# Turning q' and k' of the last four pairs with the DMA crossbar instead of TensorE

## Chip, cores, metric

One core of a Trainium2 chip. The metric is the device time of one execution in microseconds (us); lower is better. Only one core runs, so there are no dies to compare, and all runs told of here are of the fast state but one of four of e6_loaded. Before: 192.79 us (median of 3, 192.6 to 192.91).

## The reference

A gated linear recurrence over 768 steps for 4 batches of 8 heads (head size 48), then a two-layer MLP (384 to 2048 to 384) with the tanh form of gelu on its 3072 rows:

```python
for t in range(S):
    state = alpha[:, :, t, :, None] * state + np.einsum('bhd,bhe->bhde', k[:, :, t], v[:, :, t])
    y[:, :, t] = np.einsum('bhd,bhde->bhe', q[:, :, t], state)
x = y.transpose(0, 2, 1, 3).reshape(B * S, H * D)
h = x @ w_in
g = 0.5 * h * (1.0 + np.tanh(c * (h + 0.044715 * h * h * h)))
out = g @ w_out
```

## The kernel before

The steps are cut into 6 chunks of 128, the batches into 2 twos: 12 "pairs" of (chunk, two batches), numbered 0 to 11. For a pair, ScalarE takes log alpha (`la`), TensorE sums it along the chunk (`cum`), ScalarE takes exponentials (`b`, `binv`), VectorE forms q' = q b (`qp`) and k' = k binv (`kp`). The kernel turns both, so that head size lies on the partitions, before TensorE forms the scores (`at`). VectorE masks them (`atm`), TensorE forms `y` (`yps`), which is copied (`x`), turned (`xT`) and goes through the MLP (`hT`, gelu into `gT`, `acc`, `ot`, store). A list scheduler in the kernel sets the order of instructions on each engine when it is built, from a table `W` of supposed durations.

```python
    TURN_QK, TURN_X = (), ()
    BUFS = dict(ca=1, yk=2, ff=4, la=3, qp=3, kp=3, b8=2, qkT=3, atm=6, x=3, ot=6, bend=6, a=4, q=4, k=4, v=6)
...
    def turn(self, u, i, which):                     # TensorE: 8 transposes for one batch's q' and k'
        ...
            for j, n in enumerate(which):
                for p in range(H // 2):
                    nc.tensor.transpose(ps[:, j, p, :], u[n + "p"][:, i, 2 * p:2 * p + 2, :].rearrange(
                        "t h d -> t (h d)"), self.ident)
    def turned(self, u, i, which): ...               # VectorE: PSUM to qkT
    def turn_dma(self, u, n):                        # the crossbar: q' or k' of both batches at once
        def emit(e):
            self.nc.sync.dma_start_transpose(
                self.qkT(u)[:, "qk".index(n)].rearrange("d i p t -> d (i p) t"),
                u[n + "p"].rearrange("t i h d -> t (i h d)"))
...
            if m in self.TURN_QK:                    # in tasks(), pair m
                tq = [s.add("turn", {"SP": W["turn"]}, P + 10, self.turn_dma(u, n), d, xbar=W["xbar_qk"]) for n, d in (("q", qp), ("k", kp))]
                owner, turned = tq[0], tq
            for j in range(2):
                ...
                at = s.add("attn", {"PE": W["attn"]}, o + 1, self.attn(u, j), turned)   # waits for all of `turned`
```

## Time and profile before

| Share of the 191.0 us span | busy | instructions |
|---|---|---|
| TensorE (matmul) | 95% | 1919 |
| ScalarE | 71% | 300 |
| VectorE | 58% | 232 |

The profile's span is about 2 us less than the time of a run (191.0 us here, 192.79 the run). The profile's lines, and how to read them, are in the prediction below. The short of it is that TensorE runs with next to no gap from about 30 us to 187 us (from 112 us on no wait of its matmuls is listed), and the DMA engines are full until about 110 us and then nearly idle (200 GB/s from 30 to 110 us, 30 GB/s from 118 to 186).

### The profile page before, as it was taken

How to read it: one execution, taken by the hardware profiler on the slowest of the kernel's cores; microseconds unless marked ns; L12 is line 12 of the kernel's file. 1: busy time of each engine (PE TensorE's matmuls, PEld its weight loads, DVE VectorE, ACT ScalarE, POOL GpSimd, SP SyncE). 2: the span in 40 equal slices, each digit the busy share in tenths (PEclk: the TensorE clock that was granted, in tenths of full speed). 3: DMA queues.
4: the chain of work that ended last, by engine and by line, in shares of the span. 5: the costliest groups of instructions: out<-in, count | busy, mean ns of one | idle time of the engine just before them, and what ended most of it. 6: DMA issues, size and time to landing. Idle time of an engine off the chain costs nothing.

```text
span 191.0 us, 4655 instructions
## 1 busy us (share of the span) xinstructions
PE 181.4 (95%) x1919; PEld 131.8 (69%) x1922; DVE 111.2 (58%) x232; ACT 135.8 (71%) x300; POOL 63.8 (33%) x67
## 2 busy tenths in 40 slices
PE   5887899999999999999999999999999999999992
PEld 1343688656687787786786786786786786785860
DVE  7268650279695794793793883892892950850000
ACT  2544989743868878878778788788688788881931
POOL 7993433896547564655502400000000000000000
PEclk9999999999999999999999999999999999999999
DMA  6999999999999999999998770200200201101101
GB/s 129 181 179 171 207 202 228 182 180 227 249 210 182 164 241 178 181 253 173 187 246 165 152 185 0 84 2 3 82 0 6 80 3 40 42 3 43 45 13 70
DMA packets 38005, 24.68 MB, mean 129 GB/s; under 512 B 27968, under 2 KB 34624, under 8 KB 37984
## 3 DMA queue, kind: packets, MB, share of 16 engines
q0 software_dynamic: 32464, 19.27, 72.5%
q1 hardware_dynamic: 5520, 5.11, 9.1%
q8 instruction: 15, 0.25, 0.6%
q14 instruction: 6, 0.05, 0.1%
HBM read 25.17 MB, written 4.72 MB: 156 GB/s over the span
## 4 chain that ended last, share of the span: by engine, by line
PE 75%; DMA 17%; POOL 4%; issue 1%; DVE 1%; ACT 1%; POOLq 0%; DVEq 0%
PE acc L412 29%; PE hT L398 28%; DMA k<-in_k_dram 9%; DMA w_out<-in_moe_w_out_dram 8%; PE qkT_ps L289 5%; PE at L325 3%; PE yps L374 2%; PE yps L371 2%; PE kv L342 2%; PE xT_ps L388 2%; PE cum L252 2%; POOL q L220 1%; PE cum L254 1%; POOL a L220 1%; POOL k L220 1%
## 5 line engine op out<-in xcount | busy, mean ns | idle before, releaser
L404 ACT ACTIVATE gT<-hT 128x256 bf16<-128x256 f32 x192 | 64.5, 385 | 16.3 <-PE hT L398 15.6
L398 PE MATMUL hT<-xT,w_in 128*128 128x256 bf16 x576 | 71.6, 273 | 0.1
L412 PE MATMUL acc<-w_out,gT 128*128 128x384 bf16 x384 | 68.6, 326 | 0.0
L398 PEld LDWEIGHTS <-w_in 128*128 128x128 bf16 x576 | 53.6, 98 | 8.1 <-issue 0.4
L412 PEld LDWEIGHTS <-gT 128*128 128x128 bf16 x384 | 35.9, 98 | 20.2
L332 DVE TENSOR_TENSOR atm<-at,ut 128x512 bf16<-128x512 f32 x48 | 30.9, 686 | 4.8 <-PE at L325 3.2
L278 DVE TENSOR_TENSOR qp<-q,b 128x768 bf16<-128x768 f32 (+1 forms) x13 | 11.6, 896 | 33.2 <-ACT b L270 33.2
L419 ACT COPY ot<-acc 128x384 f32<-128x384 f32 x16 | 7.7, 478 | 19.0 <-PE acc L412 19.0
L220 POOL DMA_DIRECT2D a<-in_alpha_dram x12 | 13.3, 1110 | 15.3 <-ACT la L241 8.8
L220 POOL DMA_DIRECT2D q<-in_q_dram x13 | 14.6, 1122 | 11.5 <-DVE qp L278 3.6
L220 POOL DMA_DIRECT2D v<-in_v_dram x13 | 14.4, 1111 | 8.0 <-PE hT L398 1.9
L303 DVE COPY qkT<-qkT_ps 128x1024 bf16<-128x1024 bf16 (+1 forms) x22 | 13.8, 663 | 5.5 <-PE qkT_ps L289 5.5
L220 POOL DMA_DIRECT2D k<-in_k_dram x13 | 14.5, 1113 | 7.3 <-DVE xT L392 2.0
L198 ACT ACT_TABLE_LOAD x10 | 12.8, 1283 | 0.9 <-PEq L627 0.7
L241 ACT ACTIVATE la<-a 128x768 f16<-128x768 f32 (+1 forms) x13 | 10.3, 794 | 3.9 <-DMA a<-in_alpha_dram 3.7
L404 ACT ACT_TABLE_LOAD x10 | 12.8, 1283 | 0.2
L270 ACT ACTIVATE b<-cum 128x768 bf16<-128x768 f32 (+1 forms) x13 | 9.9, 762 | 4.1 <-PE cum L254 3.7
L207 PE MATMUL idle<-zero 128*128 128x512 bf16 x31 | 11.2, 483 | 1.4 <-DVE zero L594 1.2
L359 DVE TENSOR_TENSOR st<-stmp,bend 64x192 bf16<-64x192 f32 x32 | 11.3, 353 | 2.1 <-ACT gT L404 0.5
L278 DVE TENSOR_TENSOR kp<-k,binv 128x768 bf16<-128x768 f32 (+1 forms) x15 | 11.7, 792 | 0.6 <-DMA k<-in_k_dram 0.5
L392 DVE COPY xT<-xT_ps 128x384 bf16<-128x384 bf16 x24 | 8.5, 354 | 5.0 <-PE xT_ps L388 5.0
L357 DVE TENSOR_TENSOR stmp<-kv,st 64x192 f32<-64x192 f32 x32 | 11.2, 351 | 0.2
(43 smaller groups left out, 166.8 us busy)
## 6 DMA issues: line engine op xcount, KB each, us to landing
out_dram<-ot SPq DMA_DIRECT2D x24, 192.0 KB, 4.0
q<-in_q_dram POOLq DMA_DIRECT2D x11, 384.0 KB, 13.1
k<-in_k_dram POOLq DMA_DIRECT2D x11, 384.0 KB, 13.0
a<-in_alpha_dram POOLq DMA_DIRECT2D x10, 384.0 KB, 13.0
v<-in_v_dram POOLq DMA_DIRECT2D x11, 192.0 KB, 12.6
w_in<-in_moe_w_in_dram POOLq DMA_DIRECT2D x4, 384.0 KB, 11.8
w_out<-in_moe_w_out_dram POOLq DMA_DIRECT2D x4, 384.0 KB, 15.2
a<-in_alpha_dram SPq DMA_DIRECT2D x1, 384.0 KB, 4.1
```

Source lines behind the costliest of these rows:

```text
L198: nc.scalar.add_instruction(mybir.InstLoadActFuncSet(name=nc.get_next_instruction_name(), act_func_set_id=i, engine=mybir.EngineType.Activ ...
L207: self.nc.tensor.matmul(ps, self.zero[:, 0:self.C], self.zero, start=True, stop=True)
L220: (nc.sync if e == "SP" else nc.gpsimd).dma_start(u[n][:, lo:hi].rearrange("t b h d -> t (b h) d"), src)
L241: self.nc.scalar.activation(u["la"][:, lo:hi, :, 0:self.D], u["a"][:, lo:hi], AF.Ln)
L278: self.nc.vector.tensor_tensor(u[n + "p"][:, lo:hi, :, 0:self.D], u[n][:, lo:hi], u["b" if n == "q" else "binv"][:, lo:hi], op=ALU.mult)
L303: self.copy(e)(t, u.pop(("T_ps", i, which)))
L332: self.nc.vector.tensor_tensor(u["atm", i][:, o], u["at", i][:, o], self.ut[:, None, :].to_broadcast([self.C, self.H // 2, self.C]), op=AL ...
L357: nc.vector.tensor_tensor(s[ps], acc, old[ps, :, fs], op=ALU.add)
L359: nc.vector.tensor_tensor(new[ps, :, fs], acc, u["bend"][ps, i, :, None].to_broadcast([64, H // 2, D]), op=ALU.mult)
L398: self.nc.tensor.matmul(h, self.w_in[:, j, nt * self.C:(nt + 1) * self.C], self.xT[c][:, j, lo:hi].rearrange("p g t -> p (g t)"), start=j ...
L404: return lambda e: self.nc.scalar.activation(self.gT[c % self.NG][:, nt, lo * self.C:hi * self.C], f.pop(("h", c, lo, nt)), AF.Gelu_apprx_ ...
L412: self.nc.tensor.matmul(f["acc", c, b], self.gT[c % self.NG][:, nt, b * self.C:(b + 1) * self.C], self.w_out[:, nt, :], start=nt == 0, sto ...
```

## The change

Intent: take the last four pairs' 64 transposes from TensorE, the bound, and give them to DMA engines that stand idle by then.

```diff
-    TURN_QK, TURN_X = (), ()
+    TURN_QK, TURN_X = (8, 9, 10, 11), ()
```

The scheduler then makes another order: it puts the scores later, where it supposes that the transfers have landed.

## The prediction

> **What bounds the kernel now.** I read first the page's busy shares and the picture in 40 slices, then the chain of work that ended last, cut to the stretches around the last pairs, then the waits, and last the timeline of one pair. The page:
>
> ```profile
> span 191.0 us, 4655 instructions
> PE 181.4 (95%) x1919; PEld 131.8 (69%) x1922; DVE 111.2 (58%) x232; ACT 135.8 (71%) x300; POOL 63.8 (33%) x67
> PE   5887899999999999999999999999999999999992
> PEclk9999999999999999999999999999999999999999
> DMA  6999999999999999999998770200200201101101
> ```
>
> TensorE is full from about slice 7 to the last one, at full clock. The DMA engines are full up to about slice 23 (110 us) and nearly idle after it. So from 110 us on an instruction taken from TensorE should be worth its issue interval, and a transfer finds free engines. Whether TensorE's busy time is useful work is another matter, so I look at the chain, here around the tenth pair (pair 9; columns: start, us, what):
>
> ```profile
> 132.91 0.08 PE cum L254 x4
> 132.98 2.62 PE acc L412 x16
> 135.60 0.33 PE hT L398 x3
> 135.93 0.89 PE qkT_ps L289 x16
> 136.83 0.65 PE hT L398 x6
> 137.48 0.33 PE at L325 x8
> ```
>
> The pieces follow one another without a gap; the 16 transposes of q' and k' hold TensorE 0.89 us, and nothing in them waits. The stretches of the table by windows over just these four groups agree (0.89, 0.90, 0.89, 0.90). In the list of waits from 112 us to the end TensorE's matmuls have no entry at all. The bound is TensorE's instruction stream, in its order.
>
> [...] This trace shows 219 ns for one from start to modelled end, but back to back they cost 0.89/16 = 56 ns each, and that is what removing one gives back. [...] The trace of before has no crossbar transfer[...]. What it has is the output store, 192 KB from the same queue: median landing time in the DMA view, under load and at rest:
>
> ```profile
> out_dram<-ot SPq DMA_DIRECT2D x1, 192.0 KB, 6.9
> ...
> out_dram<-ot SPq DMA_DIRECT2D x2, 192.0 KB, 1.9
> ```
>
> The first is from 92 to 100 us, with loads running; the second from 140 to 160 us. Pair 8's q' is made at 119.7 us in the timeline, after the loads have drained, so all four pairs fall into the second state.
>
> **The change part by part.** *Removed from TensorE:* four pairs of 16 transposes, 0.89 + 0.90 + 0.89 + 0.90 = 3.58 us, all on the path: 192.79 - 3.58 = 189.21 us if nothing else moves. *Removed from VectorE:* eight evictions of 681 ns, 5.4 us. VectorE is 58% busy, so this is worth nothing by itself; in exchange it takes some output copies from ScalarE in the new order. *Added:* two transfers of 256 KB for each pair on SyncE's queue, which otherwise issues only stores (332 ns each). *Moved:* both halves of a pair now wait for both transfers, so the scheduler puts the scores (at) later. In the built order of the changed kernel, pair 8 has cum, 16 acc, 3 hT, 8 kv, 33 hT, then at.
>
> The budget of the transfer, from the timeline of pair 8:
>
> ```profile
> 116.74 0.84 ACT L241 ACTIVATE la<-a 128x768 f16<-128x768 f32 x1
> ...
> 118.86 0.81 ACT L270 ACTIVATE b<-cum 128x768 bf16<-128x768 f32 x1
> ...
> 119.71 0.96 DVE L278 TENSOR_TENSOR qp<-q,b 128x768 bf16<-128x768 f32 x1 [2.29 <-ACT b L270]
> ...
> 120.58 0.95 DVE L278 TENSOR_TENSOR kp<-k,binv 128x768 bf16<-128x768 f32 x1
> ```
>
> q' is ready at 120.67, k' at 121.53. The cum ends at 118.83. By the new order TensorE reaches at after acc 2.62 + hT 0.33 + kv 0.45 + hT 33 x 0.109 = 3.60, so at 125.83. The crossbar has 5.16 us from q', 4.30 us from k'. Pair 9: y 0.37 + xT 0.17 + acc 0.65 + xT 0.17 + acc 2.62 + hT 0.33 + kv 0.45 + hT 3.60 = 8.36 us after cum; but VectorE first has two x (0.56), two xT (0.36) and an output copy (0.56) to do, the last xT being ready at +1.36, so q' is done at about +3.5: 4.9 us left. Pairs 10 and 11 have no kv but 39 hT (4.25): 8.23 - 3.5 = 4.7 us left.
>
> [...] The scheduler's own table supposes 4.95 us, which tells how closely it has placed the scores, not how long a transfer takes. I charge 0.3 us in all for pairs 9 to 11.
>
> *A second small wait:* the next pair's cum. It needs la, which comes after the last gelu and a table load. In before la ends at 117.58, 2.57 us after the last hT (115.01), and cum starts 3.31 us after it: 0.74 us of slack. In the new order only acc 0.65 + at 0.33 + y 0.37 + acc 1.30 = 2.65 us lie between, so the slack is 0.08 us[...]. I charge 0.1 us for each of pairs 9, 10 and 11. Sum: 189.21 + 0.3 + 0.3 = 189.8 us, 1.6% less.
>
> **Rivals.** *A, the crossbar is late:* the wait on the transfers replaces the transposes. Each us that both transfers take over about 4.9 costs nearly 4 us in all, since TensorE takes its instructions in order and the at of every pair stands in the stream. At 6 us, 193.6; the gain is lost at 5.8 us. [...] *B, nothing shows:* ScalarE becomes the bound, because 12 hT groups now run without other matmuls between. In the tail of before 16 gelus take 5.25 us beside 48 hT of 5.24 us, so both go at one rate and B costs only the few tenths already charged. *C, load collisions:* a transfer issued under load would take about 7 us, as the store did, and cost 2 us for a pair. The last load is issued at 108.06 and the engines fall silent near 114 us; the four pairs come later, so I give it little. *D, more than the transposes is gained,* by an emptier VectorE. TensorE has no waits on VectorE after 112 us that could go, so time under 188.9 us has no source that I can see.
>
> **Range and chances.** The floor is the full removal, 189.2, with 0.2 for spread: low 189.0. The upper end is rival A with each pair 0.9 us over budget: 189.2 + 3.6 + 0.3 = 193.1, rounded to 193.0. Two per cent less is 188.93, below the floor, so faster gets 0.05. Two per cent more is 196.65, which takes a crossbar of about 6.8 us a pair: 0.08. Within 2%: 0.87.
>
> **What would show it.** Right: L289 falls from 192 to 128 transposes; eight transfers of 256 KB on SyncE's queue land in 2 to 4.5 us; PE's waits on them are under 0.3 us a pair; the PE line keeps its 9s; the at of pair 8 starts about 7.0 us after its cum ends. The cum wait would show as PE waiting for ACT la by about 0.1 us, three times. Wrong: at starts later than 8.5 us after the cum, with DMA qkT as the releaser, gaps of equal size in all four pairs (rival A) or only in the first (C); or gT as the releaser of acc or hT (B). I would be most wrong if SyncE needs several us to issue one transfer, since k' queues behind q' and the stores behind both.

The sum came to 189.8 us: 192.79 less 3.58 for the transposes, plus 0.3 for late transfers in pairs 9 to 11, plus 3 x 0.1 for the cum's waits. Both charges stand as estimates; so does "land in 2 to 4.5 us" among the signs (the eight took 3.1 to 5.0). Rival A rests on TensorE keeping its order. The trace of the changed kernel shows that: TensorE stood for 0.79 us before pair 8's scores, with 12 hT behind them, while ScalarE sat idle for 1.24 us waiting for those hT.

## The result

The changed kernel took 190.34 us (median of 4, 190.03 to 190.5) beside 192.69 us for the kernel before on the same chip; the ratio is 0.9878 (95% interval 0.9858 to 0.9898). Ratios here are the mean of one kernel's runs over the mean of the other's runs of the same rounds, so they are not quite the ratios of the medians. Executions over 1.5% slower than the fastest of the same kernel are left out of the means. Results are correct. Run again on another chip it took 190.04 us (190.03 to 190.44), ratio 0.9869 (0.9857 to 0.9882).

The page of the changed kernel, the lines that answer to those of before:

```profile
span 188.2 us, 4536 instructions
PE 177.0 (94%) x1858; PEld 127.4 (68%) x1858; DVE 109.6 (58%) x231; ACT 133.1 (71%) x293; POOL 63.7 (34%) x67
PE   5778899999999999999999999989999999999992
DMA  6999999999999999999999790290350430701101
```

TensorE's line keeps its 9s except for one slice, the 27th (122 to 127 us), and the DMA line has new work from there on. The 27th slice is pair 8. The chain of work there (start, us, what), and then the same place of pair 9:

```profile
122.00 4.29 DMA qkT<-kp
126.28 0.05 issue
126.33 0.40 PE at L325 x8
...
135.74 0.34 PE kv L342 x8
136.08 3.60 PE hT L398 x33
139.69 0.33 PE at L325 x8
```

In pair 8 the chain runs through the transfer of k', and the scores start when it lands. In pair 9 the scores follow the last hT at once, but by a margin of only 0.2 us: its k' landed at 139.47. The waits from 112 us on (engine, line, what was waited for: us in total, times, longest):

```profile
PEld L325 <- DMA qkT<-kp: 1.3, 2, 1.1
PE at L325 <- DMA qkT<-kp: 0.8, 1, 0.8
```

One wait of TensorE, 0.8 us (0.79 in the timeline), in pair 8 alone. The transfers themselves are in SyncE's timeline (start, us of issue), pairs 8 and 10:

```profile
120.55 1.35 SPq L308 DMA_TRANSPOSE qkT<-qp  x1
122.00 1.34 SPq L308 DMA_TRANSPOSE qkT<-kp  x1
...
147.72 1.24 SPq L308 DMA_TRANSPOSE qkT<-qp  x1
149.05 1.29 SPq L308 DMA_TRANSPOSE qkT<-kp  x1
```

and in the DMA view (us from the start of the issue to landing), first for 120 to 127 us, then for 147 to 153 us:

```profile
qkT<-qp SPq DMA_TRANSPOSE x1, 5.0
qkT<-kp SPq DMA_TRANSPOSE x1, 4.3
...
qkT<-qp SPq DMA_TRANSPOSE x1, 3.2
qkT<-kp SPq DMA_TRANSPOSE x1, 3.1
```

So the pair that is late issued its transfers no later than the others after its cum (q' 1.9 us after it, pairs 9 and 10 3.0 us); they took 1.2 to 1.8 us longer. To see where the time of the whole kernel went, I measured in every profile the **stretch** from the start of the last cum group of pair 8 to the start of the last output copy, which leaves out the head of the kernel (its loads differ by some tenths from run to run) and its end: before 187.33 - 118.75 = 68.58 us, changed 184.53 - 118.56 = 65.97 us. That is 2.61 us less, where 3.58 us of transposes went: 0.79 us is the wait, 0.18 us the rest.

**Why one pair of four?** Each packet on the DMA queues is in the trace. Between 121.8 and 125.8 us, two things fall together: the 2,048 packets of 256 bytes of q' and k', and at 123.5 us one packet of 16,384 bytes on the queue that the page calls "instruction" (q8). The 17 packets of the transfer that were in flight then took 1,271 to 1,552 ns, against some 20 ns in the mean otherwise, and from 124.0 to 125.2 us hardly any started. (The q8 packet itself ended at 124.5 us; why the hold outlasts it, no run shows.) These packets go with TensorE's instructions (matmuls and weight loads): from the start of one to the start of the next, TensorE starts 198 to 292 of them in the trace of before and 210 to 296 in that of the changed kernel, 251 in the mean in both; of ScalarE's it is 14 to 26, of VectorE's 4 to 18. The page of before has 1919 + 1922 = 3,841 instructions of TensorE and 15 such packets, that of the changed kernel 3,716 and 14. So I take them for fetches of TensorE's instructions, and call them fetches from here on; the trace names the queue, not the engine. Pair 9 was hit too, by a fetch at 134.9 us, and kept its scores in time by the 0.2 us above. My theory after the result, called F: **the gain is 4 x 0.89 us, less a wait in pair 8 that TensorE's own instruction fetch causes by holding the crossbar transfer for 1.2 us or more.** The rivals: U, a loss spread over all pairs (the transfers slow TensorE or VectorE while they run); S, pair 8 is late for a reason of the queue, such as the store behind it.

### The profile page after: what moved, and what is told of

It is laid out like the page before. It is cut to its first block, busy times and chain, and to the rows that moved or that the text cites. A ratio compares the mean times of both kernels' runs of the same rounds, so it can differ in the third digit from the quotient of the medians.

```text
span 188.2 us, 4536 instructions
## 1 busy us (share of the span) xinstructions
PE 177.0 (94%) x1858; PEld 127.4 (68%) x1858; DVE 109.6 (58%) x231; ACT 133.1 (71%) x293; POOL 63.7 (34%) x67
## 4 chain that ended last, share of the span: by engine, by line
PE 72%; DMA 16%; POOL 6%; ACT 1%; issue 1%; DVE 1%; POOLq 0%; DVEq 0%
PE acc L412 29%; PE hT L398 26%; DMA w_out<-in_moe_w_out_dram 8%; DMA a<-in_alpha_dram 6%; PE at L325 4%; PE qkT_ps L289 3%; DMA qkT<-kp 2%; PE yps L371 2%; PE yps L374 2%; PE cum L252 2%; PE xT_ps L388 2%; POOL w_in L228 2%; PE kv L342 1%; POOL q L220 1%; POOL v L220 1%
## 5 line engine op out<-in xcount | busy, mean ns | idle before, releaser
L398 PE MATMUL hT<-xT,w_in 128*128 128x256 bf16 x576 | 69.9, 273 | 0.4 <-DMA w_in<-in_moe_w_in_dram 0.2
L412 PE MATMUL acc<-w_out,gT 128*128 128x384 bf16 x384 | 69.4, 326 | 0.0
L419 ACT COPY ot<-acc 128x384 f32<-128x384 f32 x13 | 6.2, 477 | 15.5 <-PE acc L412 15.5
L381 DVE CAST x<-yps 128x384 bf16<-128x384 f32 x14 | 7.8, 556 | 9.3 <-PE yps L374 9.3
L207 PE MATMUL idle<-zero 128*128 128x512 bf16 x34 | 10.2, 423 | 1.2 <-DVE zero L594 1.2
L325 PE MATMUL at<-qkT 64*128 64x128 bf16 x192 | 9.5, 219 | 1.3 <-DMA qkT<-kp 0.8
```

The source lines that it names most:

```text
L207: self.nc.tensor.matmul(ps, self.zero[:, 0:self.C], self.zero, start=True, stop=True)
L325: nc.tensor.matmul(at[:, o, p, :], t[sl, 1, p, :], t[sl, 0, p, :], start=True, stop=True)
L398: self.nc.tensor.matmul(h, self.w_in[:, j, nt * self.C:(nt + 1) * self.C], self.xT[c][:, j, lo:hi].rearrange("p g t -> p (g t)"), start=j ...
L412: self.nc.tensor.matmul(f["acc", c, b], self.gT[c % self.NG][:, nt, b * self.C:(b + 1) * self.C], self.w_out[:, nt, :], start=nt == 0, sto ...
```

## The experiments

Twelve runs of ten kernels (two of them twice, and the changed kernel again), in four sets of rounds on four chips, each set beside the kernel before (192.47 to 192.6 us). Times of different sets are best compared by their ratios and stretches.

### One pair less: e1_three and e1_again

```diff
-    TURN_QK, TURN_X = (8, 9, 10, 11), ()
+    TURN_QK, TURN_X = (9, 10, 11), ()
```

> Only pairs 9, 10 and 11 by the crossbar, pair 8 back on TensorE. Theory F (the whole loss against 3.58 us sits in pair 8, whose transfer was held up by a 16 KB instruction fetch for some 1.4 us and made TensorE wait 0.79 us): pair 8 gained only about 0.1 us, so three pairs give nearly as much as four: 190.0 to 190.5 us, with no wait of scores on a transfer over 0.3 us unless a fetch falls into another pair's transfers. Rival U (each pair loses about 0.25 to 0.3 us of its 0.89[...]): three quarters of the gain of 2.35 us, so 190.9 us.

Measured: 189.43 us (189.29 to 189.73), ratio 0.9842, faster than all four pairs and faster than F had said. The stretch is 184.18 - 118.20 = 65.98 us, the same as with four pairs (65.97): as F says, the fourth pair brought nothing. But the kernel as a whole was better by more than that, so I ran it again.

> The three-pair kernel once more. It was 0.6 us faster than the four-pair kernel, while from pair 8's cum to the end of the last matmul both took the same time; the rest lay before that (0.35 us) and after the last matmul (0.35 us), where the two programs do the same. If those were chance: a ratio of about 0.986, near the four-pair kernel's 0.9869, and 118.1 to 118.3 us at pair 8's cum. If three pairs alone really are better: 0.984 again.

Measured: 189.65 us, ratio 0.9848 (0.9835 to 0.9862); the stretch is 65.97 us again. The head was chance (pair 8's last cum group at 118.52 this time, 118.20 the first). The end was not: from the start of the last output copy to the end of the span the three-pair kernel took 3.32 and 3.35 us, the four-pair kernel 3.71 and 3.69, the kernel before 3.70. The end of the trace shows why. SyncE goes through nine waits there in a fixed order, 62 ns apart, most of them for completion semaphores of its DMAs. SyncE has issued 31 DMAs in the three-pair kernel, 33 in the four-pair one and 25 before. In the three-pair kernel the wait that the last store ends is the eighth of nine, with one still to do; in the others it is the second, with seven still to do: six times 62 ns is 0.37 us. That is read from the trace; no run tests it alone.

### Moving the fetch: e2_shift

```diff
-            for _ in range(n):
-                self.nc.tensor.matmul(ps, self.zero[:, 0:self.C], self.zero, start=True, stop=True)
+            for h in (0, 256) * n:
+                self.nc.tensor.matmul(ps[:, h:h + 256], self.zero[:, 0:self.C], self.zero[:, 0:256], start=True, stop=True)
```

> All four pairs by the crossbar, as changed. Each of the idle matmuls at the start (512 columns) is cut into two of 256 columns: 34 more matmuls and 34 more weight loads, in time in which TensorE is idle. TensorE's stream is then 68 instructions longer before pair 8, so each of its 16 KB instruction fetches ([...]some 11 us apart) comes about 3.8 us earlier, at about 119.8 us instead of 123.5, and so before pair 8's transfers start moving data (121.8). Theory F: pair 8's k' lands 3.1 to 3.3 us after its issue instead of 4.3, TensorE's wait of 0.79 us goes, 189.5 us (0.6 to 0.8 less than the changed kernel). Rival S (the output store queued just behind k', or the queue itself, held the transfer): nothing of that is changed, the wait stays, 190.3 us.

Measured: 189.5 us (189.24 to 189.69), ratio 0.9844. The fetch came at 117.6 us, 5.9 us earlier in place of 3.8, so the count of instructions alone does not fix its moment. The chain at pair 8 and the DMA view from 119 to 128 us:

```profile
121.54 0.34 PE kv L342 x8
121.88 3.60 PE hT L398 x33
125.49 0.33 PE at L325 x8
```

```profile
qkT<-qp SPq DMA_TRANSPOSE x1, 3.3
qkT<-kp SPq DMA_TRANSPOSE x1, 3.1
```

The scores follow the hT at once, k' lands in 3.1 us, and the stretch is 183.62 - 118.51 = 65.11 us: 3.47 of the 3.58 us are there. The transfers, the store behind them and the order of all other instructions are as in the changed kernel, so S falls.

### Fetch moved further: e8_hit

The same cut, but in three of 170 columns.

> As the experiment with the cut idle matmuls, but cut in three: 68 more matmuls and weight loads before pair 8 in place of 34. From the fetches seen there, those of this kernel should come at about 115, 129, 140.5, 152 and 162.5 us: past pairs 8, 9 and 10, and into the transfers of pair 11 (161 to 164 us). Theory F: the transfers of pair 8 land in 3.1 to 3.3 us without a wait; k' or q' of pair 11 takes 4.3 to 5 us and TensorE waits 0.3 to 0.8 us there; 189.7 to 190.1 us. If the cut idle matmuls helped in another way than by moving the fetch: no transfer is late, 189.5 us. If pair 8 is late for a reason of its own: its wait of 0.8 us is back.

Measured: 189.64 us, ratio 0.9843, stretch 65.11 us, no late transfer. My aim was off: the fetch came at 164.9 us, after pair 11's transfers (data 161.2 to 164.0), so the hit I wanted did not happen. It only says again that without a fetch in the way there is no wait; this time in the same rounds as the second run of the changed kernel, which took 190.04 us (190.03 to 190.44) beside 189.64 (189.52 to 189.72). The hits elsewhere came unasked in other kernels. Read from the packets of every pair whose transfers fell after the loads, e7_x left out, whose other transfers have packets of the same size: the time from the first 256-byte packet of q' to the last one of k'.

| Kernel | pair | fetch starts, us | data, us |
|---|---|---|---|
| changed, two runs | 8 | 123.5, 123.3 | 3.93, 3.98 |
| changed, two runs | 9 | 134.9, 134.8 (just before the data) | 3.36, 3.55 |
| changed, two runs | 10, 11 | none | 2.75 to 2.79 |
| e1_three, e1_again | 9, 10, 11 | none | 2.76 to 2.80 |
| e2_shift, e8_hit | 8 to 11 | none | 2.75 to 2.84 |
| e3_later, e3_again | 8, 9 | 123.4, 123.7; 135.2, 135.5 | 3.87, 3.97; 3.71, 3.53 |
| e3_later, e3_again | 10, 11 | none | 2.76 to 2.78 |
| e4_early | 8 | 123.1 | 3.97 |
| e4_early | 9, 10, 11 | none | 2.75 to 2.78 |
| e5_both | 8 | 123.6 | 4.07 |
| e5_both | 9, 10, 11 | none (one in the last 0.1 us of pair 11) | 2.76 to 2.78 |
| e6_loaded | 9, 10 | 161.2; 172.3 (before the data) | 4.17; 3.71 |
| e6_loaded | 8, 11 | none | 2.81, 2.79 |
| e9_seven | 8, 9 | 128.8; 141.6 | 4.01; 4.06 |
| e9_seven | 10, 11 | none | 2.87, 2.79 |

Without a fetch 2.75 to 2.87 us, with one 3.36 to 4.17 us, for pairs 8, 9 and 10 alike and at different times. That is F's mechanism beyond the one pair.

### Same transfers, later scores: e3_later and e3_again

```diff
- xbar_qk=1500
+ xbar_qk=2500
```

(in the table `W`; it changes the order alone.)

> As changed, but the scheduler's table supposes a transfer 1 us longer, so that three more groups of hT stand before pair 8's scores: TensorE reaches them 7.85 us after the cum instead of 6.87; for pairs 9 to 11 the place stays within 0.1 us. Theory F: k' of pair 8 lands 7.6 us after the cum, so the wait goes and 0.6 to 0.8 us are saved: 189.6 us. Rival U (a loss spread over all pairs): 190.3 us.

Measured: 189.25 us (189.12 to 189.29), ratio 0.983 (0.9816 to 0.9843). Its second run on another chip:

> The kernel with pair 8's scores one us later, on the same chip as the three-pair kernel, to compare the two: its stretch from pair 8's cum to the last matmul was 0.95 us shorter than the four-pair kernel's. Expected 0.983 again, 189.3 us, and 0.5 to 0.9 us less than the three-pair kernel if that one's head and tail were chance, 0.2 us less if not.

Measured: 189.39 us, ratio 0.9834 (0.982 to 0.9847), 0.26 us below the median of the three-pair kernel in the same rounds, which fits the 0.2 us that I had set for the case that the end of that kernel is no chance. The chain of e3_again at pair 8:

```profile
122.03 4.58 PE hT L398 x42
126.62 0.33 PE at L325 x8
```

The fetch still hits (data 3.97 us), but 42 hT stand in front where 33 did, and TensorE reaches the scores after the landing. The stretch is 183.51 - 118.48 = 65.03 and 183.69 - 118.67 = 65.02 us, 3.55 and 3.56 of 3.58 us. This version beats both the kernel before and the changed one. U falls here and with e2_shift: no loss is left to spread.

### Same transfers, earlier scores: e4_early

```diff
- landed=2200, xbar_qk=1500
+ landed=1200, xbar_qk=500
```

> As changed, but the scheduler's table supposes a transfer 2 us shorter in all (1 us in landing, 1 us in the crossbar), so TensorE reaches each pair's scores 5.56 us after its cum. Without a fetch in the way k' lands about 6.5 us after the cum (q' issued at +1.9, k' at +3.35, 3.1 us to landing). The theory that each us of lateness is paid by each pair: waits of about 1.0 us in each of four pairs, more where a fetch falls in, so 189.5 + 4 = 193.5 us, range 192.9 to 195. If the transfers were hidden anyway, or if a later wait absorbed the lateness: 190.3 us.

Measured: 193.91 us (193.41 to 195.69), ratio 1.009. The waits from 112 us on:

```profile
PEld L325 <- DMA qkT<-kp: 5.7, 4, 2.4
PE at L325 <- DMA qkT<-kp: 4.6, 4, 2.2
```

Four waits, 4.6 us in all, the longest in pair 8 where the fetch hits as well. The stretch is 188.18 - 118.30 = 69.88 us, 3.9 us more than the changed kernel's; its waits are 3.8 us more (4.6 against 0.8). What comes late is paid in full, and nothing later gives it back.

### Transfers beside the old work: e5_both

TensorE and VectorE keep all their transposes; the transfers are issued too, into a tile that nothing reads.

```diff
-                self.qkT(u)[:, "qk".index(n)].rearrange("d i p t -> d (i p) t"),
+                self.extra(u)[:, "qk".index(n)].rearrange("d i p t -> d (i p) t"),
-                owner, turned = tq[0], tq
+                extra, tq = tq, []
-                if m not in self.TURN_QK:
+                if True:
+            tq += extra if m in self.TURN_QK else []
```

> TensorE and VectorE do the transposes of all pairs as in the kernel before, in the same order of instructions; the crossbar transfers of pairs 8 to 11 are issued as well, into a tile that nothing reads. This measures what the transfers cost by their presence alone. Theory F: nothing, 192.7 us. Rival U[...]: 0.2 to 1 us more than before, 192.9 to 193.7.

Measured: 192.73 us, ratio 1.0005 (0.999 to 1.002); the stretch is 187.10 - 118.52 = 68.58 us, to the digit that of before. From 118 to 186 us TensorE is busy 68.00 us in both and VectorE 33.86 and 33.85. The transfers by themselves cost TensorE and VectorE nothing that shows. U falls directly.

### Under load: e6_loaded

```diff
-    TURN_QK, TURN_X = (8, 9, 10, 11), ()
+    TURN_QK, TURN_X = (6, 7, 8, 9, 10, 11), ()
```

> Pairs 6 and 7 by the crossbar as well; their transfers fall at about 92 us and 106 us, while the loads still keep the DMA engines 70 to 100% busy. 1.79 us more come off TensorE. If load does not matter: 188.5 to 188.9 us. If transfers suffer as the stores do (6.9 us to landing at 92 to 100 us, 4.6 us at 100 to 106, against 1.9 at rest): k' of pair 6 lands about 3.3 + 8 us after its cum against a place at 6.87, a wait of 3 to 5 us, and pair 7 waits 0.5 to 3 us: 192 to 196 us.

Measured: 214.8 us (median of 4, 212.82 to 218.04, the slowest of them, which the ratio leaves out), ratio 1.1109, far outside what I had expected. The DMA view for 90 to 118 us:

```profile
qkT<-qp SPq DMA_TRANSPOSE x1, 12.1
qkT<-kp SPq DMA_TRANSPOSE x1, 16.7
```

Pair 6 waited 13.8 us, and all pairs together 23.0 us. SyncE's issue of k' alone took 6.77 us, against 1.3 at rest. My 8 us from the stores were too few. In proportion the transfers suffered no more than the stores of that stretch: 12.1 and 16.7 us are 3.8 and 5.2 times the 3.2 us at rest, and the two stores, 8.5 and 12.0 us (the second queued behind the transfers), 4.5 and 6.3 times 1.9 us. The 256 KB go as 1,024 packets of 256 bytes for each transfer, the store of 192 KB as 128 of 1,536 bytes; whether the number of packets matters is not tested. After the long wait TensorE's clock was down too: 0.55 of full between 110.9 and 115.5 us.

### Load moved away: e9_seven

```diff
-    TURN_QK, TURN_X = (8, 9, 10, 11), ()
+    TURN_QK, TURN_X = (7, 8, 9, 10, 11), ()
- xbar_qk=1500
+ xbar_qk=2500
- a=4, q=4, k=4, v=6
+ a=5, q=5, k=5, v=6
```

> Pair 7 by the crossbar too, with one more buffer each for a, q and k (5), so that the last loads are issued earlier and are drained before pair 7's transfers at about 106 us, and with the longer supposed transfer, so that the scores stand later. If load was what held pair 6 and 7 for 17 and 12 us: pair 7 lands in 3.1 to 5 us, another 0.89 us is gained over the four-pair kernel with later scores, 188.4 us (2.1% less than before). If the loads still run at 106 us: a wait of several us in pair 7, 190 to 197 us.

Measured: 194.29 us (193.83 to 195.03), ratio 1.0095. The last load was issued at 99.7 us but took 14.0 us to land, so loads still ran at 106 us; q' and k' of pair 7 took 8.0 and 8.9 us and TensorE waited 4.4 us. An earlier issue did not drain the loads in time: issued 8.4 us before its time in the kernel before (108.06), the last one still landed at 113.7, about when the engines fell silent there (near 114 us). Whether such loads are bound by their data or by their issue, no run tests. With 4.4 us the wait leaves some 1.5 us of the difference from 188.4 us, which I did not follow.

### x turned as well: e7_x

```diff
-    TURN_QK, TURN_X = (8, 9, 10, 11), ()
+    TURN_QK, TURN_X = (8, 9, 10, 11), (8, 9, 10, 11)
```

> As changed, and x of the last four pairs is turned by the crossbar too: 24 more transposes of 56 ns and 8 small evictions go, 1.34 us less on TensorE, 189.0 us if all land in time[...]. Against it: eight more transfers stand in SyncE's queue in order, each with 1 us or more of issue, and a fetch that falls into one holds it 1.4 us; then 189.5 to 191 us, with layer 1 waiting for xT.

Measured: 192.3 us (192.09 to 192.56), ratio 0.9984, worse than I had said. The two transfers of x stand before the next pair's q' in SyncE's queue and occupy it for 3.3 us (130.96 to 134.24; a transfer of x landed 3.0 us after its issue began, in the median); q' of pair 9, ready at 133.30, is issued at 134.97, a store after them. Layer 1 now waits for xT too: from 118 us on TensorE's matmuls wait 1.5 us for k', 0.5 us for xT and 1.0 us for gelu. The stretch is 67.59 us, against 65.97 less 1.34 if all had been in time. The waits listed explain part of that; the rest I did not follow.

### The changed kernel again: after_again

> The changed kernel once more, beside new runs of the kernel before, because three pairs alone had come out faster (ratio 0.9842) than all four had on another chip (0.9878), though from pair 8's cum to the last matmul both profiles take 66.0 us. If the profile is right: a ratio of about 0.986, 189.7 to 190.3 us, and again a wait of 0.6 to 0.9 us on pair 8's k', with a fetch of instructions at about 123.5 us. If the fourth pair really costs 0.9 us: 0.988 again.

Measured: 190.04 us, ratio 0.9869, stretch 184.58 - 118.45 = 66.13 us, with a wait of 0.9 us in pair 8 and its fetch at 123.3 us. The wait belongs to the program, not to the run.

## Why the prediction was right, and where not

- **TensorE's order is the bound, and 3.58 us come off it: right.** With the wait gone the stretch fell by 3.47 us (e2_shift) and 3.55 us (e3_later).
- **Price of a transpose, 56 ns back to back (0.89/16), and not the 219 ns from its start to its modelled end: right.** At 219 ns, 64 transposes would have been 14.0 us.
- **The transfers' time.** The estimate rested on a rate that no run of this case shows, and is cut; its main figure was too small. Measured: k' of pair 10, undisturbed, landed at 152.15, 4.5 us after q' was ready. The issue of a transfer took 1.24 to 1.35 us on SyncE in the changed kernel (1.86 and 2.04 us for q' of pair 9 in the two runs of the changed kernel, where a fetch fell into the issue), against 0.33 us for a store, which is what I had reckoned with for the issue. The two transfers of 262,144 bytes took 2.75 us, which is 191 GB/s, 1.4 us a transfer and 172 ns a block of 128x128; in the DMA view of the changed kernel from 119 to 128 us they move at about 190 to 220 GB/s while undisturbed, a store at up to 403.
- **Charge of 0.3 us for late transfers in pairs 9 to 11: misplaced and too small.** Pairs 9 to 11 had none. Pair 8, which had the widest budget by my sum and was charged nothing, waited 0.79 us. The term failed because it took the crossbar to have the DMA engines to itself after the loads; the changed kernel's trace has five fetches on queue q8 from 118 us on, of 0.92 to 0.96 us each. The kernel before showed a sign of it: its q8 row, 15 packets, 0.25 MB, which I had read past. What the runs show in its place: wherever a fetch falls into a pair's data or just before them (the last 0.1 us of pair 11 in e5_both apart), these take 0.6 to 1.4 us longer (3.36 to 4.17 us against 2.75 to 2.87), and pair 8 was the one whose budget did not cover it.
- **Charge of 0.3 us for the cum's wait on la: too much.** No such wait is in the list; the first cum group takes 0.19 us in pairs 9 to 11 in place of 0.16, so at most 0.03 us a pair.
- **Sum.** 0.6 us were charged, 0.97 us lost in the stretch. The result, 190.34 us, is 0.5 us above 189.8. That it comes so near is partly luck: neither charge stood for what was lost, and 0.6 us for two waits that did not come covered most of one that I had not thought of.
- **Rivals A and C, a part of each.** As in A, the scores waited for the transfer, and A's law (what is late is paid in full) is confirmed by e4_early. But the gap stood in the first pair only, which the prediction had named as the sign of C, a collision on the DMA engines. It was one, with an instruction fetch and not with the loads. B and D left no trace: in the changed kernel no wait of TensorE's matmuls on `gT` is listed, and no stretch fell by more than the 3.58 us of the transposes.
- **Rival C was right that load matters and wrong in size:** "about 7 us as the store did, and cost 2 us for a pair" measured 12 to 17 us and up to 13.8 us of waiting.

## What to carry to other kernels

Work taken from the bound engine was worth its issue interval here (64 transposes of 56 ns: 3.55 of 3.58 us came back in e3_later), provided that whatever replaces it arrives before the engine gets there (0.79 us of waiting in pair 8, 4.6 us in e4_early); leave a margin of a us or two of other work, not of a few tenths, since one fetch of instructions held a crossbar transfer that long here (1.2 to 1.8 us more to landing in pair 8). When one of several equal transfers is late, look in the packets for what else ran on the DMA engines at that moment. Use the crossbar where the DMA engines are really idle: beside loads the same transfer took up to some five times as long (16.7 us against 3.2).
